# Threshold attention and an ELU layer on one core: 37 score tiles masked on ScalarE, smaller feed-forward pieces, one scheduled block, a new order of the first 45 steps

## The chip, the core and the metric

The kernel runs on one core of one Trainium2 chip. The core has TensorE (PE in the profile; its weight loads are PEld), VectorE (DVE), ScalarE (ACT), GpSimd (POOL) and SyncE (SP), whose queue issues nearly all DMAs. The metric is the device time of one execution in microseconds (us); lower is better. Times in a profile are counted from its first instruction.

## The reference

The inputs are `q`, `k`, `v` of shape (8, 8, 576, 64) in float32, a scalar `tau`, and two weight matrices of 512 x 2048 and 2048 x 512, which arrive in float64.

```python
scores = scale * np.matmul(q, k.transpose(0, 1, 3, 2))
thresh = np.max(scores, axis=-1, keepdims=True) - tau
scores = np.where(scores >= thresh, scores, -1000000000.0)
attn = np.exp(scores - np.max(scores, axis=-1, keepdims=True))
attn = attn / (np.sum(attn, axis=-1, keepdims=True) + 1e-09)
x = np.matmul(attn, v)            # to (4608, 512): batch x position, head x dim
h = x @ w_in
g = np.where(h > 0.0, h, np.exp(np.minimum(h, 0.0)) - 1.0)
out = g @ w_out
```

So each row of scores keeps only what lies within `tau` of its maximum, and a feed-forward layer with an ELU follows.

## The kernel before, in words

**Tiles.** The 64 heads are taken in 32 pairs (`pr`), each pair in five steps `i`: four blocks of 128 query rows for two heads, and a tail step (`i == NC`) that holds the last 64 rows of both heads and counts as one head. A score tile is 128 x 576 in PSUM, in two halves of 288.

**Two blocks.** The first 45 steps (pairs 0 to 8, 81 score tiles) are built by `early_tasks` in one block with an order written out by hand (`tc.manual_schedule()`). The other 23 pairs and most of the feed-forward work follow in a second such block, whose order comes from a clock of its own (`on_pe`, `at`). The second block forms its products by a scheme with seven products for eight (L1466 and L1606).

**One step of the first block.** `scores` (L551, PE) fills the PSUM tile. `max_of` (L600, DVE) takes the negated row maximum. `bound_of` (L604, POOL) makes the threshold. `exp_of` (L614, ACT) writes exp(score - max) to SBUF. `mask_of` (L623, DVE) compares the PSUM tile with the threshold, multiplies by the exponential, writes the weights `w` and adds up their row sum. `total_of` (L631, DVE; L590, ACT, for the steps in `SU_ACT`) and `reciprocal_of` (L637, DVE) give 1/sum, and the weights are scaled on POOL (`normalize`, L596) or, for the heads in `ACT_NORM`, on ACT (L584). The PSUM tile is free after the mask; from step 10 on (`LATE`) there are two tiles, so that each score waits for the masks of the step before.

**Turning.** The weights must be transposed for the product with `v`. Either PE does it in nine 128 x 128 blocks (L640; six in a tail step) with copies on ACT (L656), or, for the steps in `SQUARES`, DVE transposes 32 x 32 squares (L716) and a trip through DRAM (`there`, then `wTa`/`wTb`, issued by SP) does the rest. `values` (L777 and L782) forms attention times `v`; `values_out` (L899) copies it to `xt`. PE also makes transposes of an identity as padding (28 at the start, 16 after the first scores, then 6 to 11 beside the blocks of steps 0, 1, 3, 5 and 7).

**Weights.** 32 pieces of float64 weights are converted: `load_w` (L408, SP), `convert_rest` (L415 on ACT, L432 on POOL for `REST_POOL`), `convert_shift` (L421, DVE), `convert_add` (L427, POOL), `convert_abs` (L437, ACT), `convert_end` (L445, DVE). Sums of `w_in` blocks for the second block are made on DVE or POOL (`make_in`, L1066; POOL for `IN_POOL`).

**Feed-forward work of the first block.** 32 units for the first 512 rows of output: `ffn1` (L940: two groups of four products, 256 columns each; then exp L947 on ACT, minus one L950 on POOL, ELU L954 on DVE) and `ffn2_plain` (L980: four products of 512 columns). Each unit is given out in two halves by `half()`.

**What sets the order.** Each job is a task with a time: a formula of its step plus two entries of the table `MOVED`, one for the kind of job and one for that single job. The jobs are carried out in the order of these times, each after the jobs that it needs (`do`), so that a job with a late time moves forward to the first job that needs it. Every engine then runs its own instructions in that order.

```python
def task(x, t, key, f, *needed):
    each = "_".join(map(str, x)) if isinstance(x, tuple) else x
    made[x] = [t + (MOVED.get(key, 0.0) if key else 0.0) + MOVED.get(each, 0.0), len(made), f, needed, False]
```

Of the kernel before, what the change touches and what calls it, by code (L numbers as in the profile page):

```python
# [18 lines left out]
ACT_NORM = {(0, 1), (10, 0), (10, 1), (11, 1), (13, 0), (15, 1), (16, 0), (17, 0), (17, 1), (18, 1), (22, 0), (24, 0), (25, 0),  # L19
 (26, 1), (28, 0), (30, 1), (31, 0), (32, 0), (33, 0), (35, 0), (36, 0), (36, 1), (37, 0), (40, 1), (44, 0), (44, 1)}  # L20
IN_POOL = {(6, 2), (1, 2), (7, 1), (0, 0), (3, 1), (6, 1), (0, 2), (5, 0), (7, 2), (2, 2), (1, 0), (4, 1), (5, 2)}
SU_ACT = {33, 41, 13, 16, 24, 30}
REST_POOL = {9, 27}

MOVED = {
# [289 lines left out]
def kernel(  # L315
# [642 lines left out]
    def hidden(c, u, n):  # L958
        half, u = divmod(u, NU // 2)
        return gs[c][half][:, u : u + n]  # L960
# [917 lines left out]
```

## Time and profile before

| what | value |
|---|---|
| median of 3 runs | 1300.2 us (1298.6 to 1300.24) |
| profiled execution: span from first to last instruction | 1298.8 us |
| mean granted TensorE clock | 0.997 |
| median of the runs less the span | 1.4 us |
| first product of the second block (L1466) | 282.14 us |
| DMA | 256.01 MB, mean 197 GB/s |

The profiled execution has no time of its own beside its span; the runs' median stands for it, 1.4 us above.

The page gives the busy time of each engine over the span, then rows of 40 slices in which a digit is the busy share in tenths. A group line names the source line, the engine, the operation, out<-in with shape and count, then the busy time, the mean time of one in ns, and the idle time of the engine just before with what ended it. A line of the timeline begins with start and length in us; in square brackets is the wait before it. The share of an engine is an average over stages, so tables of stretches are read beside it: the first block lies in 0 to 282 us.

| 0 to 282 us | PE | DVE | ACT | POOL |
|---|---|---|---|---|
| busy, us | 268.5 | 222.0 | 168.4 | 179.7 |

### The profile page before, as it was taken

Reading aid. Unit: us, or ns where it says so; the run is one execution under the profiler, and the core shown is the slowest. Engines: PE = TensorE matmul, PEld = TensorE weight load, DVE = VectorE, ACT = ScalarE, POOL = GpSimd, SP = SyncE. Lnnn points to the kernel's source line nnn. Section 1 sums busy time; section 2 is a strip of 40 time slices with the busy share of each in tenths; the row PEclk is TensorE's granted clock in tenths of the full one; section 3 lists DMA queues with packets and bytes.
Section 4 is the critical chain, followed back from the end, with each engine's and each line's share of the span. In section 5 each row is a group of like instructions: output and inputs, shape, how many; then the busy total and the mean of one; then the engine's idle time right before and its main releaser. Section 6 shows DMA issues by size and latency. Waiting matters only on the chain.

```text
span 1298.8 us, 21747 instructions
## 1 busy us (share of the span) xinstructions
PE 1277.1 (98%) x6822; PEld 993.8 (77%) x6822; DVE 1011.8 (78%) x2199; ACT 567.9 (44%) x1224; POOL 790.9 (61%) x1181
## 2 busy tenths in 40 slices
PE   9999999899999999999999999999999999999998
PEld 7676576446878888878878787878787888888887
DVE  6787887788888988898889889897989882545534
ACT  5888644335262525353444444353525261421320
POOL 4686645767476756766576757574867473524533
PEclk9999999899999999999999999999999999999999
DMA  7546377879898988899889888899899875222211
GB/s 149 129 146 191 97 192 207 250 203 267 210 255 223 269 226 242 236 269 225 237 214 250 240 235 223 254 245 240 227 255 256 229 214 169 89 73 63 92 61 33
DMA packets 327827, 256.01 MB, mean 197 GB/s; under 512 B 209312, under 2 KB 288672, under 8 KB 327712
## 3 DMA queue, kind: packets, MB, share of 16 engines
q1 hardware_dynamic: 325776, 254.14, 72.1%
q8 instruction: 54, 0.88, 0.3%
q10 hardware_dynamic: 1936, 0.48, 0.2%
q14 instruction: 61, 0.50, 0.1%
HBM read 165.94 MB, written 88.60 MB: 196 GB/s over the span
## 4 chain that ended last, share of the span: by engine, by line
PE 82%; DVE 4%; DMA 2%; issue 1%; POOL 1%; ACT 1%; SPq 0%; DVEq 0%; ACTq 0%; POOLq 0%
PE f L1606 30%; PE f L1466 28%; PE sc L829 7%; PE sc L889 7%; PE f L980 3%; PE sc L551 2%; PE f L940 1%; PE sc L881 1%; DMA there<-x 1%; PE pv L782 1%; PE sc L876 1%; DVE x L716 1%; PE rt L640 1%; DVE w L623 1%; DMA sw<-win_sums 1%
## 5 line engine op out<-in xcount | busy, mean ns | idle before, releaser
L596 POOL TENSOR_SCALAR w<-w,rs 128x576 f32<-128x576 f32 x172 | 141.4, 830 | 78.0 <-DVE rs L637 73.3
L836 DVE TENSOR_REDUCE mx<-sc 128x1 f32<-128x576 f32 x207 | 148.2, 749 | 29.6 <-PE sc L829 25.8
L846 ACT ACTIVATE w<-sc,mx 128x576 f32<-128x576 f32 x115 | 82.9, 740 | 117.9 <-DVE mx L836 99.9
L1466 PE MATMUL f<-xt,sw 128*128 128x256 f32 x512 | 123.9, 384 | 1.4 <-ACT xt L899 0.8
L1466 PE MATMUL f<-xt,w_in_sb 128*128 128x256 f32 x512 | 122.3, 381 | 0.1
L842 POOL TENSOR_SCALAR th<-mx,ntau 128x2 f32<-128x2 f32 (+1 forms) x115 | 34.3, 298 | 136.6 <-DVE mx L836 136.6
L716 DVE STREAM_TRANSPOSE x<-w 128x512 f32<-128x512 f32 (+2 forms) x163 | 106.9, 690 | 11.8 <-POOL w L596 10.6
L1466 PEld LDWEIGHTS f<-xt,sw 128*128 128x128 f32 x512 | 93.6, 190 | 21.6 <-issue 4.9
L1466 PEld LDWEIGHTS f<-xt,w_in_sb 128*128 128x128 f32 x512 | 96.2, 190 | 15.9 <-ACT w L1480 2.8
L1466 PE MATMUL f<-x,w_in_sb 128*128 128x256 f32 x448 | 106.1, 379 | 1.3 <-ACT g L1527 1.3
L1606 PE MATMUL f<-w_out_sb,g 128*128 128x256 f32 x448 | 107.1, 382 | 0.0
L1606 PE MATMUL f<-w_out_sb,s 128*128 128x256 f32 x448 | 107.0, 382 | 0.0
L1606 PE MATMUL f<-t,s 128*128 128x256 f32 x448 | 105.8, 379 | 0.0
L829 PE MATMUL sc<-kT,qT 64*128 64x448 f32 (+4 forms) x736 | 103.2, 416 | 0.5 <-DVE w L850 0.5
L829 PEld LDWEIGHTS sc<-kT,qT 64*128 64x128 f32 x736 | 80.6, 186 | 25.5 <-issue 16.8
L1553 POOL TENSOR_TENSOR s<-g 128x256 f32<-128x256 f32 x104 | 80.4, 778 | 29.3 <-PE f L1606 20.0
L850 DVE SCALAR_TENSOR_TENSOR w<-sc,th,w 128x576 f32<-128x576 f32 x115 | 89.7, 810 | 10.2 <-ACT w L846 10.1
L1466 PEld LDWEIGHTS f<-x,w_in_sb 128*128 128x128 f32 x448 | 85.0, 190 | 13.3 <-ACT g L1527 1.7
L1606 PEld LDWEIGHTS f<-w_out_sb,g 128*128 128x128 f32 x448 | 84.1, 190 | 14.2 <-issue 3.2
L1606 PEld LDWEIGHTS f<-w_out_sb,s 128*128 128x128 f32 x448 | 84.2, 190 | 13.5 <-issue 2.5
L1606 PEld LDWEIGHTS f<-t,s 128*128 128x128 f32 x448 | 85.1, 190 | 11.6
L596 POOL TENSOR_SCALAR e<-e,rs 128x576 f32<-128x576 f32 x92 | 68.5, 748 | 35.5 <-DVE rs L637 33.4
(209 smaller groups left out, 2831.5 us busy)
## 6 DMA issues: line engine op xcount, KB each, us to landing
there<-x SPq DMA_DIRECT2D x436, 144.0 KB, 3.6
wTb<-there SPq DMA_DIRECT2D x56, 576.0 KB, 6.5
wTa<-there SPq DMA_DIRECT2D x53, 576.0 KB, 4.9
sw<-win_sums SPq DMA_DIRECT2D x62, 384.0 KB, 4.3
t<-wout_sums SPq DMA_DIRECT2D x45, 512.0 KB, 5.8
qm<-in_q_dram SPq DMA_DIRECT2D x124, 72.0 KB, 4.8
vm<-in_v_dram SPq DMA_DIRECT2D x64, 128.0 KB, 3.7
wst<-in_moe_w_in_dram SPq DMA_DIRECT2D x16, 512.0 KB, 4.4
```

The lines of the kernel that those rows point to most:

```text
L596: nc.gpsimd.tensor_scalar(wv, wv, st["rs"][:, h : h + 1], 1.0, ALU.mult, ALU.mult)
L716: nc.vector.transpose(x[:, :, c0 : c0 + nc_], src.rearrange("p (c g n) -> p g c n", c=nc_, n=T))
L829: on_banks(nc.tensor.matmul(o, qT[r, i * P : (i + 1) * P], kT[r, k0 : k0 + n], start=True, stop=True, skip_group_check=True), o)
L836: on_banks(nc.vector.tensor_reduce(st["mx"][:, h : h + 1], st["sc", h], axis=AX.XY if i == NC else AX.X, op=ALU.max, negate=True), st["sc" ...
L842: nc.gpsimd.tensor_scalar(st["th"][:, cs], st["mx"][:, cs], -1.0, ntau, ALU.mult, ALU.add)
L846: on_banks(nc.scalar.activation(st["e", h], st["sc", h], AF.Exp, bias=st["mx"][:, h : h + 1]), st["sc", h])
L850: on_banks(nc.vector.scalar_tensor_tensor(st["e", h], st["sc", h], st["th"][:, h : h + 1], st["e", h], ALU.is_ge, ALU.mult, accum_out=st[" ...
L889: on_banks(nc.tensor.matmul(o, vm[:, h, c], parts[part][:, g0:g1, h * (NC + 1) + c], start=False, stop=(c == NC - 1), skip_group_check=Tru ...
L980: nc.tensor.matmul(cur[c, i][:, :DM], hidden(c, ft % NU, 1)[:, 0, ft // NU, i], w_out_sb[:, ft], start=(ft == 0), stop=(ft == NFT - 1))
L1466: nc.tensor.matmul(loc["banks"][place], left[:, j], right[:, j], start=(begins and j == 0), stop=(j == 1), skip_group_check=True)
L1553: engine.tensor_tensor(o, x, y, op)
L1606: nc.tensor.matmul(place(m), lhs, rhs, start=(begins and v == 0), stop=(v == RU - 1), skip_group_check=True)
```

## The change

Sizes of the sets, counted over heads or pieces that exist:

| set | before | after |
|---|---|---|
| `MASK_ACT`: heads masked on ACT | none | 37 of 81 |
| `ACT_NORM`: heads scaled on ACT | 24 | 38 |
| `SU_ACT`: steps summed on ACT | 6 | 12 |
| `REST_POOL`: low words on POOL | 2 | 17 of 32 |
| `SHIFT_POOL`: shifts on POOL | none | 7 of 32 |
| `IN_POOL`: weight sums on POOL | 13 | 14 |
| `SQUARES`: steps turned through DRAM | 17 | 18 (step 22 is new) |

- A head in `MASK_ACT` has no exponential, bound and mask of the old kind. `pivot_of` (DVE) writes th = -max + tau, limited to 104, for each row. `sink_of` (ACT) writes a parametric relu of score + th to SBUF: what is below zero is multiplied by 2^126. `raise_of` (ACT) takes exp(that - tau) in place and adds up the row sum, so that the sunk elements become zero. The next user of the PSUM tile waits for `sink_of`, not for the mask.
- `ffn1` and `ffn2_plain` hand out four parts instead of two; each old place for a half now holds two jobs, `half` and `rest_half`, which move separately.
- The two-head steps turned through DRAM use two DVE transposes (five and four blocks) instead of three.
- The loads of pair 1 leave the start job and become jobs of their own.
- The second block's code moves into the first `manual_schedule` block.
- `MOVED` is new for the jobs of the first block; its entries for the second block are equal in both kernels.
- Code for turning q and k on PE (`QK_PE`) is added, with an empty set: it does nothing.

```diff
+SHIFT_POOL = {0, 2, 3, 4, 13, 24, 29}
+QK_PE = set()
+    DEEP = 104.0
+    STEEP = 2.0**126
...
-        nc.vector.tensor_scalar(ntau, ntau, -1.0, None, ALU.mult)
-        nc.vector.tensor_scalar(ntau0, ntau, 1.0 / SCALE, None, ALU.mult)
+        nc.vector.tensor_scalar(ntau0, ntau, -1.0 / SCALE, None, ALU.mult)
+        nc.vector.tensor_scalar(ntau, ntau, DEEP, -1.0, ALU.min, ALU.mult)
...
-            nc.vector.tensor_scalar(top, hi, 3, None, ALU.logical_shift_left)
+            if i in SHIFT_POOL:
+                nc.gpsimd.tensor_tensor(top.bitcast(I32), hi.bitcast(I32), eight.broadcast_to([P, WN]), ALU.mult)
+            else:
+                nc.vector.tensor_scalar(top, hi, 3, None, ALU.logical_shift_left)
...
+    def pivot_of(pr, i, h):
+        st = open_steps[pr, i]
+        mx, th = st["mx"][:, h : h + 1], st["th"][:, h : h + 1]
+        if pr:
+            nc.vector.tensor_scalar(th, mx, ntau, None, ALU.subtract)
+        else:
+            nc.vector.tensor_scalar(th, mx, keep, ntau, ALU.mult, ALU.subtract)
+
+    def sink_of(pr, i, h):
+        st = open_steps[pr, i]
+        wv = weights_of(st)[:, h * S : (h + 1) * S]
+        nc.scalar.activation(wv.rearrange("p (a n) -> p a n", a=2), st.pop(h)[:, :, :HALF], AF.Prelu,
+                             bias=st["th"][:, h : h + 1], scale=1.0 if pr else keep, alpha=STEEP)
+
+    def raise_of(pr, i, h):
+        st = open_steps[pr, i]
+        wv = st["w"][:, h * S : (h + 1) * S]
+        nc.scalar.activation(wv, wv, AF.Exp, bias=ntau, accum_out=st["sm"][:, h, :1])
...
-        if i < NC and pr >= JOINED:
+        if i < NC:
             turn_part(0, w[:, : (NC + 1) * P], NC + 1)
             turn_part(NC + 1, w[:, (NC + 1) * P :], NC)
-        elif i < NC:
-            turn_part(0, w[:, :MAIN], NC)
-            turn_part(NC, w[:, MAIN : MAIN + P], 1)
-            turn_part(NC + 1, w[:, MAIN + P :], NC)
...
-        def part(k):
+        def part(x):
+            k, j0 = x // 2, x % 2 * 2
             ft = 2 * u + k
-            if k == 0:
+            if x == 0:
                 loc["ph"] = bank()[:, : 2 * CT].rearrange("p (k t) -> p k t", k=2)
-            for j in range(KJ):
+            for j in range(j0, j0 + 2):
...
-        return [lambda: run(0), lambda: run(1)], (done, no, no) if 4 * part + 4 == NFT else (no, no, no)
+        return [lambda k=k: run(k) for k in range(4)], (done, no, no) if 4 * part + 4 == NFT else (no, no, no)
...
             load(0, ("v",))
-            load(1)
             idle(28)
...
-            rooms += [("mask", n, h) for h in hs]
+            rooms += [("exp" if (n, h) in MASK_ACT else "mask", n, h) for h in hs]
...
                         task(("half", n, x, y), t + u, f"half{x}{k}", half)
+                        task(("rest_half", n, x, y), made["half", n, x, y][0] + 0.001, None, half, ("half", n, x, y))
...
     with tc.manual_schedule():
         early_tasks()
-    assert progress[0] == len(pieces) and not units and not pending
-    with tc.manual_schedule():
+        assert progress[0] == len(pieces) and not units and not pending
         need_extra("in")
```

More of the change, by code (lines that the diff above doesn't have):

```diff
@@ L398 @@
     staged, tops = {}, {}
+    eight = const.tile([P, 1], I32, name="eight")
+    nc.gpsimd.memset(eight, 8)
     progress = [0]
@@ L460, in load @@
             m = tiles[name]
+            if pr in QK_PE:
+                if "ends" not in tiles:
+                    tiles["ends"] = wstage.tile([TAIL, 2, 2, D], FP32, name="ends", bufs=1)
+                both, blocks = src[b, 2 * j : 2 * j + 2], blocks_of(pr, name[0])
+                for i in range(2):
+                    queue.dma_start(blocks[:, :, i], both[i, :MAIN].rearrange("(c p) d -> p c d", p=P))
+                queue.dma_start(tiles["ends"][:, int(name == "km")], both[:, MAIN:].rearrange("i p d -> p i d"))
+                continue
             for i, d in pieces:
@@ L479, in load_v, with room_q @@
             nc.sync.dma_start(vd[r, r], vh[MAIN:])
-    def prep_q(pr):
+    def room_q(pr):
         if pr < 2:
@@ L495, in prep_k, with blocks_of, turn_blocks, turn_last @@
     def prep_k(pr):
-        kT = pairs[pr][1] = firsts[pr] if pr < 2 else qkp.tile([P, TAIL + S], FP32, name="kT")
+        kT = room_k(pr)
         nc.vector.transpose(kT[:, TAIL:], raws[pr]["km"].rearrange("p j d -> p (j d)"))
+    def blocks_of(pr, name):
+        return raws[pr][name + "m"].rearrange("p j d -> p (j d)")[:, :MAIN].rearrange("p (c i d) -> p c i d", i=2, c=NC)
+    def turn_blocks(pr, name):
+        rt, src = psum["t"].tile([P, NC, P], FP32, name="rt", tag="rt"), blocks_of(pr, name)
+        for c in range(NC):
+            transpose(rt[:, c], src[:, c].rearrange("p i d -> p (i d)"))
+        return rt
+    def turn_last(pr):
+        rt, ends = psum["t"].tile([P, NC, P], FP32, name="rt", tag="rt"), raws[pr]["ends"]
+        for x in range(2):
+            nc.tensor.matmul(rt[:, x, :TAIL], ends[:, x], idents[-1][:TAIL, :TAIL], is_transpose=True, skip_group_check=True)
+        return rt
+    def copy_blocks(pr, name, rt):
+        rt = rt.rearrange("p c n -> p (c n)")
+        if name == "q":
+            nc.scalar.mul(room_q(pr)[:, :MAIN], rt, keep)
+        else:
+            nc.scalar.copy(room_k(pr)[:, TAIL:S], rt)
+    def copy_last(pr, rt):
+        qT, kT, _ = pairs[pr]
+        nc.scalar.mul(qT[:, MAIN:], rt[:, 0, :TAIL], keep)
+        nc.scalar.copy(kT[:, S:], rt[:, 1, :TAIL])
     def copy_q(pr):
@@ L954, in elu @@
             nc.vector.scalar_tensor_tensor(loc["g"], loc["g"], 0.0, loc["ph"], ALU.min, ALU.max)
-        return [lambda: part(0), lambda: part(1)], (exp, minus, elu)
+        return [lambda x=x: part(x) for x in range(4)], (exp, minus, elu)
     def hidden(c, u, n):
@@ L978, in run @@
                 cur[c, i] = bank()
-            for ft in range(4 * part + 2 * k, 4 * part + 2 * k + 2):
-                nc.tensor.matmul(cur[c, i][:, :DM], hidden(c, ft % NU, 1)[:, 0, ft // NU, i], w_out_sb[:, ft],
-                                 start=(ft == 0), stop=(ft == NFT - 1))
+            ft = 4 * part + k
+            nc.tensor.matmul(cur[c, i][:, :DM], hidden(c, ft % NU, 1)[:, 0, ft // NU, i], w_out_sb[:, ft],
+                             start=(ft == 0), stop=(ft == NFT - 1))
         def done():
@@ L1184, in early_tasks @@
             made["prep", x, 0] = made["copy", x, 0] = made["start"]
-            made["load", x, 1] = made["start"]
-        made["v", 0] = made["v", 1] = made["start"]
+            task(("load", x, 1), -99.0, None, lambda x=x: load(1, (x + "m",)), "start")
+        made["v", 0] = made["start"]
+        task(("v", 1), -98.0, None, lambda: load(1, ("v",)), "start")
         task("rest", begin[0] + 0.5, "restq", rest_of_q, "start")
@@ L1190, in early_tasks @@
         made["v", 2] = made["v", 3] = None
+        turned = {}
         for pr in range(1, NPAIR + 6):
@@ L1290, in early_tasks @@
-                exps.append(("exp", n, h))
                 back = ("turned", n - (2 if last_ else WBUFS)) if n >= WBUFS else None
-                task(("mask", n, h), at_(2.0 + 1.6 * h, 5.6 + 0.1 * h, 4.0 + 0.1 * h), f"mask{h}{k}", lambda pr=pr, i=i, h=h: mask_of(pr, i, h),
-                     ("exp", n, h), ("th", n, h), ("mask", n, 0) if h else back, "late" if last_ else None)
+                t_exp, t_th, t_mask = (at_(0.3 + 0.7 * h, 2.0 + 0.6 * h, 1.0 + 0.5 * h), at_(0.4 + 0.7 * h, 2.2 + 0.6 * h, 1.1 + 0.5 * h),
+                                       at_(2.0 + 1.6 * h, 5.6 + 0.1 * h, 4.0 + 0.1 * h))
@@ new lines, in early_tasks @@
+                if (n, h) in MASK_ACT:
+                    task(("exp", n, h), t_exp, f"exp{h}{k}", lambda pr=pr, i=i, h=h: sink_of(pr, i, h), ("th", n, h), back, "late" if last_ else None)
+                    task(("th", n, h), t_th, f"th{h}{k}", lambda pr=pr, i=i, h=h: pivot_of(pr, i, h), ("max", n, h))
+                    task(("mask", n, h), t_mask, f"mask{h}{k}", lambda pr=pr, i=i, h=h: raise_of(pr, i, h), ("exp", n, h))
+                else:
+                    task(("exp", n, h), t_exp, f"exp{h}{k}", lambda pr=pr, i=i, h=h: exp_of(pr, i, h),
+                         ("max", n, h), exps[-1] if exps else None, ("mask", *exps[-2][1:]) if len(exps) > 1 else None)
+                    task(("th", n, h), t_th, f"th{h}{k}", lambda pr=pr, i=i, h=h: bound_of(pr, i, h), ("max", n, h))
+                    exps.append(("exp", n, h))
+                    task(("mask", n, h), t_mask, f"mask{h}{k}", lambda pr=pr, i=i, h=h: mask_of(pr, i, h), ("exp", n, h), ("th", n, h),
+                         ("mask", n, 0) if h and (n, 0) not in MASK_ACT else back, "late" if last_ else None)
```

65 lines of the change are left out of this document (46 added, 19 removed), and 581 rows, old and new, of the table MOVED.

## The prediction

> **What bounds the kernel now.** I read the head of the page first, then the table of stretches, then the timeline where a stretch was not full.
>
> ```profile
> span 1298.8 us, 21747 instructions
> PE 1277.1 (98%) x6822; PEld 993.8 (77%) x6822; DVE 1011.8 (78%) x2199; ACT 567.9 (44%) x1224; POOL 790.9 (61%) x1181
> ...
> PE   9999999899999999999999999999999999999998
> ...
> PEclk9999999899999999999999999999999999999999
> ```
>
> TensorE (PE) is busy 98% of the span, and the two slices below 9 are the eighth (its clock dips there too) and the last. So a gain must come from TensorE time that is idle, slow or filled with padding. The stretches (columns: span; busy time of PE, PEld, DVE, ACT, POOL; clock; DMA share; GB/s) say where that is:
>
> ```profile
> 0.00:60.00 60.00, 56.16 (x388) 42.43 (x389) 45.19 (x106) 39.23 (x75) 33.46 (x68) 1.00 0.67 140
> 60.00:220.00 160.00, 157.24 (x800) 103.69 (x799) 128.66 (x283) 108.80 (x223) 99.13 (x147) 1.00 0.59 167
> 220.00:282.00 62.00, 55.05 (x204) 25.31 (x202) 48.19 (x111) 20.41 (x35) 47.06 (x71) 0.94 0.82 222
> 282.00:320.00 38.00, 35.49 (x172) 26.01 (x172) 33.58 (x73) 20.82 (x48) 28.50 (x43) 1.00 0.89 243
> 320.00:1298.80 978.80, 973.10 (x5263) 796.41 (x5262) 756.16 (x1629) 378.68 (x846) 582.79 (x856) 1.00 0.74 202
> ```
>
> The changed job list runs from 0 to 282 us, where the first L1466 product starts. By busy time TensorE is idle there only 3.8 + 2.8 + 7.0 = 13.6 us. But matmul records overlap: in an unbroken run of the timeline 56 products of 256 columns take 12.29 us, 0.219 each, while one record lasts 0.38. So I counted work by the pace from start to start: L980 128 x 0.43 = 55.0; L940 256 x 0.216 = 55.3; scores 36 x 1.17 + 9 tail steps x 0.97 = 50.8; values 44.4 (9 x 1.88 and 8 x 2.30 for L782, 9.2 for L777); turned blocks 234 x 0.109 = 25.5; first L876 1.2. That is 232.2 us of work in 282.1: **49.9 us are not work**. Of these 14.4 are the 132 padding transposes at 0.109 (28 of them before any score), some 3 the half clock at 242.6 to 249.4, and about 32 gaps: some 9 in 0 to 60 (4 of them the start), 10 in 60 to 220, 13 in 220 to 282. No other engine is full: over 0 to 282 DVE is busy 222, ACT 168, POOL 180.
>
> The largest gap:
>
> ```profile
> 238.07 1.24 PE L551 MATMUL sc<-kT,qT 64*128 64x288 f32 x8
> ...
> 243.31 2.26 PE L551 MATMUL sc<-kT,qd 128*128 128x288 f32 x4 [4.00 <-DVE w L623]
> ```
> ```profile
> 239.00:243.30 4.30, 0.31 (x4) 0.02 (x1) 3.79 (x8) 2.05 (x3) 2.90 (x6) 0.92 0.99 333
> 243.30:249.00 5.70, 5.69 (x9) 3.06 (x10) 4.12 (x12) 0.74 (x1) 5.25 (x6) 0.50 0.89 198
> ```
>
> Scores of step 38 are followed at once by those of step 39, whose PSUM tile is freed by the mask (L623) of step 38, 5.0 us after its scores began. TensorE waits 4.0 us, and then its granted clock is 0.50 for the next 5.7 us. The price of this one place is 4.0 + some 3 = **7 us**.
>
> **The change, part by part.** Durations:
>
> ```profile
> L623 DVE SCALAR_TENSOR_TENSOR w<-sc,th,e 128x576 f32<-128x576 f32 x81 | 63.7, 812 | 18.2 <-ACT e L614 9.6 <-POOL th L604 6.8 <-POOL qd L504 0.6
> L614 ACT ACTIVATE e<-sc,mx 128x576 f32<-128x576 f32 x72 | 51.2, 742 | 37.7 <-DVE mx L600 37.6
> L427 POOL TENSOR_TENSOR wtop<-wtop,wst 128x512 int32<-128x512 int32 x32 | 42.8, 1338 | 11.0 <-DVE wtop L421 5.7 <-ACT wTb L656 1.9 <-ACT wst L415 1.2
> L604 POOL TENSOR_SCALAR th<-mx,ntau 128x1 f32<-128x1 f32 x81 | 24.2, 303 | 30.7 <-DVE mx L600 30.2
> L421 DVE TENSOR_SCALAR wtop<-wst 128x512 uint32<-128x512 uint32 x32 | 16.9, 538 | 0.1
> L584 ACT ACTIVATE w<-w,rs 128x576 f32<-128x576 f32 x24 | 18.5, 774 | 17.5 <-DVE rs L637 15.2 <-DMA km<-in_k_dram 2.3
> ```
>
> *37 masks on ScalarE.* Each drops a DVE mask (0.812 and its accumulator read 0.083) and a POOL bound (0.303); it adds a DVE pivot (128x1, as L379: 0.155) and a second ACT pass. No row shows Prelu; I take L614's 0.742 for it, the same shape from PSUM; ends are 0.59 (L947, 128x512) and 0.83 (L614 of the first pair, with a scale from memory). The Exp in SBUF I take as L584's 0.774, up to 1.06 if a read of the accumulator as long as L590's 0.29 comes with it. DVE: 37 x (0.155 - 0.895) = -27.4. POOL: -11.2. ACT: 37 x 0.774 = +28.6 (ends +23 and +43).
> *Shifted between engines.* ACT_NORM grows from 24 real heads to 38: ACT +14 x 0.774 = +10.8, POOL -14 x 0.843 = -11.8. Fifteen more low words on POOL: ACT -15 x 0.687 = -10.3, POOL +15 x 0.673 = +10.1. Seven shifts: DVE -3.8, POOL +9.4 (as L427; 0.7 to 1.5 each as ends). Six more sums on ACT, one more weight sum on POOL: DVE -1.4, ACT +1.8, POOL +0.8.
> *Squares.* One more step (22) is turned through DRAM: TensorE -9 x 0.109 = -1.0, ACT -1.4, DVE +1.5, four more stores and one fetch while the DMA share is 0.6. Two transposes for three in the 14 two-head steps: DVE 14 x (0.838 + 0.682 - 1.635) = -1.6.
> Sums over 0 to 282: DVE 222 to 189, ACT 168 to 198 (192 to 212), POOL 180 to 177. This work lies beside TensorE, so none of it counts by itself. Cover: TensorE's 232 us; without it, ACT's 198 would be the longest. What counts is when PSUM and turned weights come free.
>
> *When PSUM comes free.* A score tile is now held through max, exp and mask; for the 37 heads only through max, pivot and Prelu. That is one pass of 0.8 us less, and no wait for the POOL bound (L623 waits 6.8 us for it in all). Queued behind a late Prelu on ACT are norms, PSUM copies (L656) and the ELU's exp; behind a late pivot, the next maxima.
>
> *Order and quarter units.* The matmuls are the same; a unit's piece is 0.86 us instead of 1.72. I sorted the jobs by the formulas and offsets of both tables. Before, no feed-forward piece stands between scores 38 and 39; after, four do (3.4 us). That leaves 0.6 of the 4.0 us and keeps the clock. After also puts two to nine pieces around nearly every score from step 10 on. Bare spots stay: only values (2.5 to 2.9 us with their first product) stand between scores 29 and 30, 34 and 35, 39 and 40, 43 and 44, and between 7 and 8.
>
> *Loads of pair 1* leave the start job; they are on SP's queue still, behind those of pair 0, and scores of step 2 start at 16.2 us: nothing (ends -1 to +1). *Single block:* the first wide score at 280.63 waited for a mask, no engine drains there: nothing (ends -2 to +2). The second block's 171 offsets are equal in both tables, so the 978.8 us from 320 on stay.
>
> **Sum.** (a) The place at 239: 7 us at most; its four pieces leave other places, so at least the clock's 3: I take 6. (b) Other gaps of 220 to 282, 5 to 6 us, every step there waiting for its predecessor's mask; 7 of the heads of steps 37 to 44 change: 1.5 (0 to 5). (c) 60 to 220, 10 us in gaps of 0.2 to 0.7: finer pieces, fewer waits for masks: 3 (0 to 8). (d) 0 to 60, 5 us and 11 of padding behind the first scores: 1.5 (0 to 8). (e) Transposes 1. Together 13, bounds 4 to 29. From the profiled span 1298.8 that gives 1285.8. The runs' median, 1300.2, lies 1.4 above the span: **1287 us**. About 0.2% (2.6 us) is what a measurement of this kernel tells from no change.
>
> **Rivals.**
> 1. *ACT takes DVE's place (17%).* In 40 to 140 ACT is busy 84 of 100 us. In steps 7 to 23 it gains 11 masks (+9.4) and 7 norms (+5.4) and loses 13 low words (-8.9): 90 of 100. As its queue is in order, PSUM copies would then come late and (b), (c), (d) vanish, 6 us: 1293. Against it: in that stretch ACT still has 10 us.
> 2. *A new bare spot (slower, 13%).* The values that alone cover scores 29-30, 34-35, 39-40, 43-44 need a fetch of 3.9 to 5.4 us to have landed; where one is late by 1 us or more, the 3.8 us from a score's end to the next free tile stay open, the clock halves, and the place costs 7 us. One or two are paid by the 13; from the third the kernel is slower; with three or four it stands at 1300.2 - 13 + 21 to 28 = 1308 to 1315. The limit of the clock lies between 1.5 us (the wait before 307.08 left it at 1.00) and 4.0. For it: exactly this happened at 239. Against it: the wait for a fetch is 0.3 us at most now. The Trainium skill, TensorE: Matmul & The Clock Gate, section Part 1, puts the limit at an idle window of about 3.4 us; by that, waits of 3.8 us would halve the clock as assumed here, while by the upper row, 4.0, such a place would cost 3.8 us alone and four would be needed.
> 3. *Prelu and Exp need different tables (slower, 3%).* The trace has one table load, 1.283 us, for Exp, Tanh and copies together. Two loads for each of 37 heads are 95 us on ACT, 200 + 95 = 295 in a stretch of 282, at a busy share of 0.9 some 328: 46 more and no gain, 1346. The Trainium skill, ScalarE: Activation LUTs, section Table sets, says that cheap functions such as relu are in every set, and that each switch costs about 2.7 us with its drain (estimate from that page: 200 us on ACT); no run here shows Prelu yet.
> 4. *More than I take (15%).* DVE's 33 us and the earlier tiles close most gaps: -20 to -25, 1275 to 1280.
> 5. *Moved, not closed (7%).* Gaps of equal size elsewhere: 1298 to 1303. That the masks do not move is excluded by the sets in the diff.
> Forecast itself: 45% (1281 to 1292, its own range). Faster by over 0.2%: 45 + 15 + 17 = 77%; within 7%; slower 16%. The range 1275 to 1308 takes in rivals 1, 4 and 5 and the near end of 2; it leaves out the rest of 2, rival 3 and gains over 25 us, some 15%.
>
> **What would show it.** The first L1466 product at about 269 us instead of 282; no stretch of half clock after the start; L623 44 times instead of 81; DVE near 189 us of that stage and ACT near 200; one table load. Wrong: a wait of TensorE over 3 us, a PE row below 9 between slices 3 and 9, or ACT over 90% where score tiles are late.

## The result and the profile after

The changed kernel takes 1289.3 us (median of 4 runs, 1288.85 to 1290.47) against 1300.1 (median of 4, 1298.6 to 1300.24): a ratio of 0.9921 with a 95% interval of 0.9907 to 0.9935, faster by 10.8 us. The forecast was 1287.0, in a range of 1275 to 1308. The profiled execution of the new kernel took 1289.09 us with a span of 1287.3; in what follows times inside a span come from such profiled executions, and ratios from the runs.

The head of the page of the new kernel, the same lines as those shown of the old one:

```profile
span 1287.3 us, 21652 instructions
...
PE   8999999989999999999999999999999999999998
...
PEclk9999999999999999999999999999999999999999
```

The clock row has no dip left, and the eighth slice is a 9; the first and the ninth are an 8 now. The stretches with the same columns as before (span; busy PE, PEld, DVE, ACT, POOL; clock; DMA share; GB/s), cut at the first product of the second block again, which is L1580 here:

```profile
0.00:60.00 60.00, 55.29 (x380) 42.12 (x381) 41.87 (x99) 41.18 (x79) 36.27 (x68) 1.00 0.60 130
60.00:220.00 160.00, 159.54 (x811) 105.40 (x810) 117.92 (x255) 128.64 (x271) 102.90 (x139) 1.00 0.67 184
220.00:271.00 51.00, 48.09 (x195) 23.00 (x194) 41.33 (x86) 29.21 (x55) 35.92 (x50) 1.00 0.86 256
...
309.00:1287.30 978.30, 972.36 (x5262) 796.09 (x5260) 755.33 (x1627) 378.76 (x845) 582.10 (x855) 1.00 0.74 202
```

The first L1580 product starts at 270.18 instead of 282.14, and from it to the end it takes 1017.1 us against 1016.7 before: everything that was gained lies ahead of it. In the first row TensorE is busy less than before (55.29 against 56.16): the start did not gain. The gap at 239 us is closed by four quarter pieces, and the step behind it follows without a wait:

```profile
232.32 1.24 PE L617 MATMUL sc<-kT,qT 64*128 64x288 f32 x8
233.49 3.70 PE L1065 MATMUL f<-w_out_sb,g 128*128 128x512 f32 x8
237.03 1.13 PE L617 MATMUL sc<-kT,qd 128*128 128x288 f32 x4
```

The groups of the mask (busy us in all, mean ns of one, then idle time before and its releasers):

```profile
L711 DVE SCALAR_TENSOR_TENSOR w<-sc,th,e 128x576 f32<-128x576 f32 x44 | 34.9, 813 | 14.2 <-ACT e L704 10.6 <-POOL th L670 2.5 <-POOL g L1035 0.3
L695 ACT ACTIVATE w<-w,ntau 128x576 f32<-128x576 f32 x37 | 28.7, 776 | 0.9
L689 ACT ACTIVATE w<-sc,th 128x576 f32<-128x576 f32 x33 | 24.3, 738 | 18.1 <-DVE th L682 11.5 <-POOL t L1178 2.9 <-DVE x L804 2.2
L682 DVE TENSOR_SCALAR th<-mx,ntau 128x1 f32<-128x1 f32 x33 | 7.0, 213 | 1.1
L695 ACT ACTIVATION_READ_ACCUMULATOR w<-w,ntau 128x1 f32 x37 | 7.0, 190 | 0.0
```

L689 is the parametric relu: 738 ns, where 742 was taken. The second pass, L695, is 776 ns plus 190 for the read of its accumulator. The pivot, L682, is 213 ns, where 155 was taken.

To see where the 12 us come from, I worked out from the traces how much TensorE time is lost in each stretch of steps: the time from one matmul's start to the next, less the shortest usual time (the tenth percentile in the old and the new kernel) for that pair of shapes. The half clock counts as lost, too. Two executions of one kernel (new and e11) differ by up to 1.1 us in a column, and another rule for pairs that are rare moves most entries by less than 0.5 us (the last of e9 by 0.9). For old and new and for the experiments below (us; the right column is the start of the first product of the second block):

| kernel | steps 0-9 | 10-22 | 23-34 | 35 to the first product | first product at |
|---|---|---|---|---|---|
| old | 12.2 | 8.8 | 6.6 | 17.9 | 282.1 |
| new | 13.0 | 5.2 | 5.6 | 9.5 | 270.2 |
| e1 code only | 11.8 | 8.8 | 6.6 | 16.4 | 281.1 |
| e2 masks alone | 21.8 | 12.1 | 19.1 | 22.9 | 312.7 |
| e3 order alone | 22.1 | 13.3 | 25.1 | 22.2 | 320.2 |
| e4 old engine split | 22.0 | 29.6 | 17.2 | 22.6 | 328.6 |
| e5 old, half moved | 12.3 | 8.5 | 6.5 | 15.1 | 279.2 |
| e6 new, bare spot | 12.3 | 5.4 | 5.4 | 14.7 | 273.8 |
| e7 whole halves | 13.9 | 12.3 | 11.2 | 11.9 | 285.7 |
| e8 early table load | 11.9 | 5.6 | 5.4 | 14.3 | 273.1 |
| e9 old, wait filled | 11.9 | 8.6 | 6.2 | 12.3 | 279.8 |
| e10 e8, end filled | 12.6 | 5.5 | 5.4 | 8.7 | 269.3 |
| e11 new again | 12.6 | 5.6 | 5.4 | 10.6 | 270.1 |
| e12 ten masks back | 21.6 | 10.2 | 5.4 | 10.7 | 283.6 |

In e9 and e10 unread transposes fill 3.5 and 1.5 us of wait; this table does not count them as lost.

### The profile page after: what moved, and what is told of

Its sections match the earlier page's. It is cut to its first block, busy times and chain, and to the rows that moved or that the text cites. A ratio compares the mean times of both kernels' runs of the same rounds, so it can differ in the third digit from the quotient of the medians.

```text
span 1287.3 us, 21652 instructions
## 1 busy us (share of the span) xinstructions
PE 1270.5 (99%) x6813; PEld 992.2 (77%) x6813; DVE 989.9 (77%) x2136; ACT 598.5 (46%) x1296; POOL 788.5 (61%) x1154
## 4 chain that ended last, share of the span: by engine, by line
PE 87%; DVE 5%; ACT 2%; DMA 2%; POOL 2%; issue 1%; SPq 1%; DVEq 0%; ACTq 0%; POOLq 0%
PE f L1720 30%; PE f L1580 28%; PE sc L913 7%; PE sc L973 7%; PE f L1025 4%; PE sc L617 3%; PE rt L728 2%; PE pv L866 2%; PE sc L965 1%; DVE x L804 1%; PE sc L960 1%; PE f L1065 1%; DMA wst<-in_moe_w_out_dram 1%; DVE mx L666 1%; DMA sw<-win_sums 1%
## 5 line engine op out<-in xcount | busy, mean ns | idle before, releaser
L662 POOL TENSOR_SCALAR w<-w,rs 128x576 f32<-128x576 f32 x158 | 127.7, 817 | 80.4 <-DVE rs L725 77.1
L1580 PE MATMUL f<-xt,sw 128*128 128x256 f32 x512 | 123.9, 384 | 1.2 <-ACT xt L983 0.5
L1580 PE MATMUL f<-xt,w_in_sb 128*128 128x256 f32 x512 | 122.3, 381 | 0.1
L804 DVE STREAM_TRANSPOSE x<-w 128x512 f32<-128x512 f32 (+1 forms) x151 | 107.6, 744 | 17.3 <-POOL w L662 16.2
L1580 PEld LDWEIGHTS f<-xt,sw 128*128 128x128 f32 x512 | 93.7, 190 | 21.3 <-issue 5.5
L1580 PEld LDWEIGHTS f<-xt,w_in_sb 128*128 128x128 f32 x512 | 96.2, 190 | 15.9 <-ACT w L1594 2.8
L1580 PE MATMUL f<-x,w_in_sb 128*128 128x256 f32 x448 | 106.1, 379 | 1.6 <-ACT g L1641 1.6
L1667 POOL TENSOR_TENSOR s<-g 128x256 f32<-128x256 f32 x104 | 80.3, 778 | 29.6 <-PE f L1720 20.1
L934 DVE SCALAR_TENSOR_TENSOR w<-sc,th,w 128x576 f32<-128x576 f32 x115 | 89.8, 811 | 10.3 <-ACT w L930 10.2
L1580 PEld LDWEIGHTS f<-x,w_in_sb 128*128 128x128 f32 x448 | 85.0, 190 | 13.5 <-ACT g L1641 2.0
L1720 PEld LDWEIGHTS f<-w_out_sb,s 128*128 128x128 f32 x448 | 84.2, 190 | 13.5 <-issue 2.5
```

The source lines that it names most:

```text
L662: nc.gpsimd.tensor_scalar(wv, wv, st["rs"][:, h : h + 1], 1.0, ALU.mult, ALU.mult)
L804: nc.vector.transpose(x[:, :, c0 : c0 + nc_], src.rearrange("p (c g n) -> p g c n", c=nc_, n=T))
L934: on_banks(nc.vector.scalar_tensor_tensor(st["e", h], st["sc", h], st["th"][:, h : h + 1], st["e", h], ALU.is_ge, ALU.mult, accum_out=st[" ...
L1580: nc.tensor.matmul(loc["banks"][place], left[:, j], right[:, j], start=(begins and j == 0), stop=(j == 1), skip_group_check=True)
L1667: engine.tensor_tensor(o, x, y, op)
L1720: nc.tensor.matmul(place(m), lhs, rhs, start=(begins and v == 0), stop=(v == RU - 1), skip_group_check=True)
```

## The experiments

### Each part by itself

**e1_code_only.** The new code with the old tables; ACT_NORM, IN_POOL, SU_ACT, REST_POOL and the order, MOVED, are those of the old kernel, too:

```diff
-MASK_ACT = {(0, 0), (0, 1), (5, 1), (7, 1), (8, 0), (9, 1), (13, 0), (15, 0), (15, 1), (16, 0), (20, 0), (20, 1), (23, 0),
...
+MASK_ACT = set()
-SHIFT_POOL = {0, 2, 3, 4, 13, 24, 29}
+SHIFT_POOL = set()
```

> The new code with the old tables: no mask on ScalarE, the old sets of engines, every second half right behind its first half, the old order of jobs, and pieces 1 and 2 of nine value groups transposed in one issue of two parts. My theory, in which the gain comes from the new order and the new split of the engines together: only the transposes are left, which I priced at 1.0 us; the time lies between the old 1300.1 and 1298.5, the wait of 4 us and the half clock at 239 us stay. Rival, that code outside the tables carries much of the gain: 1296 or less.

Measured: 1302.83 us, ratio to the old kernel 1.0014 (1.0005 to 1.0022), slower than either expectation. VectorE's two transposes for three bring nothing: from step 2 to step 39 no step starts more than 0.2 us from its old place, and scores 39 start at 243.3 us as in the old kernel. The 1.0 us that the expectation speaks of is not tried here: the prediction put it on the nine blocks of step 22 that TensorE no longer turns, and with the old tables e1 turns step 22 on TensorE as before (1388 matmuls ahead of the second block, as in the old kernel; the new one has 1379). What the profile shows ahead of the second block (1.1 us) comes behind step 39, where the half clock lasted 3.41 us instead of 6.83; and the second block takes 1.8 us longer than in the old kernel, half of it in its first 300 products. So the code outside the tables carries none of the gain.

**e2_masks_alone, e3_order_alone, e4_old_engine_split.** Three ways to take the change apart. e2 is e1 with the new set of 37 masks left in. e3 is the new kernel with this edit:

```diff
-MASK_ACT = {(0, 0), (0, 1), (5, 1), (7, 1), (8, 0), (9, 1), (13, 0), (15, 0), (15, 1), (16, 0), (20, 0), (20, 1), (23, 0),
...
+MASK_ACT = set()
```

e4 is the new kernel with ACT_NORM, IN_POOL, SU_ACT and REST_POOL of the old one and

```diff
-SHIFT_POOL = {0, 2, 3, 4, 13, 24, 29}
+SHIFT_POOL = set()
```

> The same old tables and old order, with the 37 masks on ScalarE alone. VectorE gets about 28 us of work less in 45 steps (813 ns each) and 37 pivots more (213 to 273 ns), ScalarE 36 us more (738 to 776 ns and a 190 ns read each). If VectorE's place in the queue was what the old order suffered from, the time falls by 2 to 6 us (1294 to 1298) with the order as it was. If the order is what counts, and the masks only move the load, the old order, made for masks on VectorE, now waits for ScalarE at places where its Exp and copies stand ahead: 1300 to 1308.

> The new order, the new sets and the quarter units, but all 90 masks on VectorE again. VectorE's load up to the first product of the second block goes from 201 to about 222 us of 270, ScalarE's from 199 to about 163. Theory that masks on ScalarE are what makes the new order possible: products wait for masks again, 1295 to 1305. Rival, that the order of TensorE's pieces alone closes the gaps and VectorE keeps up: within 1.5 us of 1289.3.

> The new kernel with the old choice of engines for normalisations, additions, sums, copies and shifts (seven shifts, fifteen of the seventeen rests back on VectorE or ScalarE); masks and order of TensorE's pieces as in the new one. Theory that the 37 masks and the order carry it: 1289 to 1293. Rival, that the freed time of VectorE is needed twice (moves to GpSimd included): more than 1294, with waits for VectorE between 150 and 270 us.

Measured: 1330.16 us, ratio 1.0221 (1.0205 to 1.0236); 1338.78, 1.0291 (1.0272 to 1.0309); 1353.66, 1.0398 (1.0383 to 1.0413). e2 and e3 end far above what was expected (1308 and 1305 at most; the expectation of e3 speaks of 90 masks, but there are 81). For e4 the rival came, more than 1294, but TensorE waited for GpSimd most of all, and not for VectorE. Against the old kernel each part without the others costs 29 to 53 us, some three to five times what all of them together gain. What TensorE waited for in the first 290 us, with the sum, the number of waits and the longest; masks alone first:

```profile
PE rt L716 <- POOL w L650: 10.1, 11, 2.9
PE sc L605 <- ACT w L677: 6.8, 4, 4.0
PE rt L716 <- ACT wTb L732: 3.8, 2, 2.0
```

the new order without the masks on ScalarE:

```profile
PE rt L726 <- POOL w L660: 14.3, 6, 6.3
PE sc L615 <- DVE w L709: 9.4, 8, 2.7
PE sc L615 <- POOL qT L530: 3.1, 1, 3.1
```

the old split of the engines:

```profile
PE rt L727 <- POOL w L661: 17.4, 12, 5.0
PE rt L727 <- ACT w L649: 4.6, 3, 2.1
```

and the new kernel itself, in its 270 us:

```profile
PE rt L728 <- POOL w L662: 1.5, 2, 1.3
PE rt L728 <- POOL ident masks.py:199: 1.5, 1, 1.5
PE sc L617 <- DVE w L711: 1.4, 2, 1.3
```

No engine is full in any of them (with the masks alone, ScalarE is busy 197 us of the 313 ahead of the second block, VectorE 200, GpSimd 167). As I read these rows, what is long is the chain from a mask to the scaled weights that the transposes (`rt`) read: mask, sum, reciprocal, scaling on GpSimd. In each variant one link of it comes at another time than the order of the queues allows for. The order was not fitted anew to any of the three, so they show what a part costs in an order made for another split, and not what it could gain in an order of its own.

**e12_ten_masks_back** shows such a place by itself, and whether the loss is made good later.

```diff
-MASK_ACT = {(0, 0), (0, 1), (5, 1), (7, 1), (8, 0), (9, 1), (13, 0), (15, 0), (15, 1), (16, 0), (20, 0), (20, 1), (23, 0),
+MASK_ACT = {x for x in {(0, 0), (0, 1), (5, 1), (7, 1), (8, 0), (9, 1), (13, 0), (15, 0), (15, 1), (16, 0), (20, 0), (20, 1), (23, 0),
...
-  0), (34, 0), (35, 1), (36, 1), (37, 0), (37, 1), (38, 1), (40, 0), (41, 0), (42, 0), (44, 0)}
+  0), (34, 0), (35, 1), (36, 1), (37, 0), (37, 1), (38, 1), (40, 0), (41, 0), (42, 0), (44, 0)} if x[0] >= 20}
```

> The new kernel with the ten masks of steps 0 to 16 back on VectorE, the other 27 on ScalarE. With all 37 back the kernel was 49 us slower, 1.3 us for each, while VectorE got only 21 us of work. Theory that a loss is local and is kept (TensorE has no slack later): some 13 us are lost by step 17, as in that run, and stay: 1300 to 1304. Rival, that the later steps catch up because their order had room: 1291 to 1296.

Measured: 1304.14 us against 1290.12 of the unchanged kernel on the same chip (ratios to the old kernel 1.0041, 1.0029 to 1.0054, and 0.9927): 14 us for ten masks, whose passes on VectorE are some 8 us. It is lost where the masks are, 2.3 us by step 8, 7.9 by step 9 and 12.6 by step 17, and it is still 13.5 at the first product of the second block: nothing is made good. GpSimd's timeline of this run, between the scores of steps 8 and 9:

```profile
47.83 0.74 POOL L662 TENSOR_SCALAR w<-w,rs 128x576 f32<-128x576 f32 x1
49.65 0.63 POOL L670 TENSOR_SCALAR th<-mx,ntau 128x1 f32<-128x1 f32 x1 [1.07 <-DVE mx L666]
50.24 0.64 POOL L456 TENSOR_SCALAR wst<-wst 128x512 f32<-128x512 uint32 x1
50.97 1.27 POOL L451 TENSOR_TENSOR wtop<-wtop,wst 128x512 int32<-128x512 int32 x1
52.23 2.71 POOL L662 TENSOR_SCALAR w<-w,rs 128x576 f32<-128x576 f32 x3
```

The same queue in the unchanged kernel (e11):

```profile
42.80 0.74 POOL L662 TENSOR_SCALAR w<-w,rs 128x576 f32<-128x576 f32 x1 [0.93 <-PE sc L617]
43.51 0.27 POOL L670 TENSOR_SCALAR th<-mx,ntau 128x1 f32<-128x1 f32 x1
43.74 0.67 POOL L456 TENSOR_SCALAR wst<-wst 128x512 f32<-128x512 uint32 x1
44.49 1.29 POOL L451 TENSOR_TENSOR wtop<-wtop,wst 128x512 int32<-128x512 int32 x1
45.77 2.20 POOL L662 TENSOR_SCALAR w<-w,rs 128x576 f32<-128x576 f32 x3
```

The jobs look alike, but the bound (L670) is another one. In the unchanged kernel it is that of step 7, whose maximum is there already. With (8, 0) masked on VectorE again, the first head of step 8 has a bound, too, and that is the one that stands ahead of the two conversions and the scalings of step 7: it waits for the maximum of step 8, which needs the scores of step 8 (47.52 us). So the scalings of step 7, whose reciprocals are there at 48.84, start at 52.23, and TensorE's timeline shows what follows:

```profile
53.55 1.31 PE L728 MATMUL rt<-ident,w 128*128 128x128 f32 x5 [3.91 <-POOL w L662]
55.32 1.54 PE L728 MATMUL rt<-ident 128*128 128x128 f32 x6 [0.46 <-ACT wTb L744]
```

From scores 8 to scores 9 it takes 11.2 us instead of 5.5, the half clock for 3.41 us behind the wait among it. By this reading one tiny instruction (0.27 us in the unchanged kernel) in the wrong place of one queue costs 5.7 us; no run moves it alone.

**e7_whole_halves.** The quarters out of the order:

```diff
-    91.1, "rest_9": 97.1, "rest_half_10_1_0": -81, "rest_half_10_2_0": -4, "rest_half_11_1_0": -1, "rest_half_11_2_0":
...
+    91.1, "rest_9": 97.1, "s13.0": -0.93,
```

All 68 entries of that kind are out, so that a half's second part follows its first.

> The new kernel with the second part of each feed-forward half right behind its first part (68 entries of the order taken out), so that the units are halves again. Theory, in which the quarter unit is a finer filling: some waits grow by up to half a piece each, 1290 to 1294. Rival, that the quarters are what closes the place at 239 us and the period of 5.1 us at scores 40 to 43: 1295 or more, with a wait of over 2 us there. Third, that they are idle detail: within 0.7 us of 1289.3.

Measured: 1302.46 us, ratio 1.0019 (1.0008 to 1.0029). The whole gain is gone. This is the second rival in size, but not by its place: the lost time of steps 35 to the first product rises by 2.4 us, and that of steps 10 to 34 from 10.8 to 23.5, where the old kernel loses 15.4. So in this order the gain of the middle steps cannot do without the quarter unit. An order made anew for whole halves was not tried.

### The place at 239 us and the clock

**e5_before_half_moved.** In the old kernel:

```diff
-    "half_38_0_0": -3.1,
+    "half_38_0_0": 1.90,
```

> The old kernel with one feed-forward half (1.72 us of products) moved from ahead of scores 38 to between scores 38 and 39, where TensorE waited 4.0 us. My theory: the wait falls to about 2.3 us, the clock record of 0.5 (6.8 us) at 242.6 us is gone, and the time falls by the 1.7 us of cover and the 3.4 us that half the clock cost, less what the earlier scores 38 lose: 1295 to 1297. Rival, that the half clock has another cause than the bare wait: the record stays and the time falls by 1.7 us at most, 1298.4 or more.

Measured: 1298.69 us against 1300.04, ratio 0.9989 (0.9979 to 1.0). In the profiled execution the wait is 2.09 us, no record of half clock follows and the first product comes 3.0 us earlier; the runs give only 1.4 us. Five of the eleven executions took 1297.07 to 1297.40 us, the profiled one among them, and six 1298.69 to 1300.9, so the 3.0 us are not what each of them gains. The mechanism of the theory is there, and its size is nearer to the rival's.

**e6_after_bare_spot.** The converse in the new kernel:

```diff
-    "post_35_1_0_1": 854.29,
+    "post_35_1_0_1": 871.79,
...
-    "post_36_1_0_2": 851.8,
+    "post_36_1_0_2": 863.40,
```

> The new kernel with the four quarter pieces (3.70 us) that stand between scores 38 and 39 moved behind scores 39, nothing else. The spot is bare again: scores 39 wait for the mask of scores 38, by its end in the new profile some 3.2 us. Theory (a bare wait of some 3 to 4 us brings half the clock for 6.8 us): a wait of 2.5 to 3.5 us, the clock record of 0.5 behind it, 1292 to 1295. Rival, that the pieces moved behind the scores fill the later gaps and the clock holds: 1289 to 1292, no record under 1.0.

Measured: 1293.12 us, ratio 0.9940 (0.9927 to 0.9952), against 0.9921 and 0.9927 (each plus or minus 0.0013) of the new kernel: some 2 us. The bare spot is back, with ScalarE's mask as its end now:

```profile
231.15 1.24 PE L617 MATMUL sc<-kT,qT 64*128 64x288 f32 x8
235.56 2.29 PE L617 MATMUL sc<-kT,qd 128*128 128x288 f32 x4 [3.18 <-ACT w L689]
237.65 5.35 PE L1065 MATMUL f<-w_out_sb,g 128*128 128x512 f32 x8
```

The wait is 3.18 us, half clock follows for 6.83 us (eight products take 5.35 us instead of 3.70), and the first product comes 3.6 us later. The moved pieces stand behind scores 39 and shorten later gaps, so 3.2 + 3.4 us did not all add up.

**e9_before_filled_wait** parts the wait from the clock. In the old kernel, ahead of scores 39:

```diff
-        return lambda: values_out(pr, part, pv)
...
+        held[:] = [pv]; return lambda: values_out(pr, part, pv)
...
-            task(("sc", n), t + 0.2 if late_ else t - 2.6 if i in (2, NC) else t - 2.0, f"sc{k}", lambda pr=pr, i=i, hs=hs: scores(pr, i, hs), ("prep", "q", pr),
+            task(("sc", n), t + 0.2 if late_ else t - 2.6 if i in (2, NC) else t - 2.0, f"sc{k}", lambda n=n, pr=pr, i=i, hs=hs: ([transpose(held[0][:, :P], idents[-1]) for _ in range(30 * (n == 39))], scores(pr, i, hs)), ("prep", "q", pr),
```

(`held` keeps the tile of the value products that was copied last; the transposes go there.)

> The old kernel with 30 transposes that nobody reads put ahead of scores 39, where TensorE waited 4.0 us bare (one takes some 0.12 us, so 3.7 us); nothing else is moved. This parts the wait from the half clock. Theory: scores 39 start at 243.3 us as before, since the mask ends when it did, but no clock record of 0.5 follows, and scores 40 start some 3.4 us earlier, at 248.1; in all 1296.5 to 1297.5. Rival, that the clock is not tied to the bare wait, or that transposes do not hold it: record and time as before, 1299.5 to 1301.

Measured: 1299.14 us against 1299.59, ratio 0.9998 (0.9989 to 1.0007): no change that the runs can tell, though the interval leaves room for a gain of 1.4 us. The wait at 239 us and what follows, in stretches of 3.41 us, with the columns of the stretches above, in the old kernel:

```profile
239.16:242.57 3.41, 0.15 (x2) 0.00 (x0) 3.06 (x6) 1.89 (x3) 2.19 (x6) 1.00 1.01 328
242.57:245.99 3.42, 2.68 (x5) 1.85 (x6) 2.04 (x7) 0.00 (x0) 3.34 (x4) 0.50 0.88 284
```

and in this run:

```profile
238.57:241.98 3.41, 3.35 (x30) 3.11 (x29) 3.28 (x6) 1.66 (x3) 2.42 (x6) 1.00 1.00 332
241.98:245.40 3.42, 2.90 (x9) 1.67 (x10) 2.29 (x8) 0.74 (x1) 3.34 (x5) 1.00 0.89 259
```

The transposes hold the clock at 1.00, as the theory has it. But what TensorE does faster runs into the next wait, as its timeline in this run shows:

```profile
242.50 1.21 PE L551 MATMUL sc<-kT,qd 128*128 128x288 f32 x4 [0.58 <-DVE w L623]
...
249.02 1.79 PE L551 MATMUL sc<-kT,qT 64*128 64x288 f32 x8 [1.27 <-DVE kT L497]
```

Scores 40 wait 1.27 us for VectorE's transposed keys. From scores 39 to scores 40 it takes 6.5 us instead of 8.2, so 1.7 of the 3.4 us that half the clock cost TensorE are left. In this execution, the shortest of the eleven, the first product of the second block comes 2.4 us earlier, 0.8 of them gained ahead of scores 39. What the runs of the old kernel show beside it agrees in size: of its 53 executions on the three chips of these experiments, the 26 with a mean granted clock of 0.997 or less took on the average 1.6 us longer than the 27 with more, each counted from the median of its chip; where the clock was halved in them is not on record. So I estimate that the half clock costs the kernel 1 to 2 us at most, and not 3.4.

### The start and the end of the stage

**e8_early_table_load.** In the start job, behind the loads:

```diff
             load(0, ("v",))
+            nc.scalar.activation(seen, ident[:, :1], AF.Exp)
             idle(28)
```

> The new kernel with one Exp of 128 by 1 elements added on ScalarE right after the loads at the start, whose output nothing uses. Theory: the load of the activation table (1283 ns), which now stands at 9.72 us behind the wait of the first parametric relu, runs during the loads of the start, the first mask ends 1.3 us earlier, and the start to scores 2 gains 0.5 to 1.3 us of which some is eaten later: 1288.0 to 1289.0. Rival, that the first steps are held by the loads of pair 1 and not by the first mask: no change, 1289.3 within 0.4.

In the new kernel the load of the activation table stands behind the wait of the first parametric relu. ScalarE's timeline of the new kernel:

```profile
9.72 1.28 ACT L689 ACT_TABLE_LOAD   x1 [9.72 <-DVE th L684]
11.01 1.55 ACT L689 ACTIVATE w<-sc,th,keep 128x576 f32<-128x576 f32 x2
```

and of this run:

```profile
9.39 1.80 ACT L689 ACTIVATE w<-sc,th,keep 128x576 f32<-128x576 f32 x2 [5.60 <-DVE th L684]
```

Measured: 1291.00 us, ratio 0.9928 (0.9916 to 0.9941), the same as without it; both expectations, 1289.7 at most, were missed. The start did gain. In the profiled executions of the new kernel and of e8, e10 and e11 the first scores start anywhere between 6.3 and 7.5 us, with the early load or without it, so I count from them: scores 2 follow after 11.2 us in e8 and e10, after 12.1 in the new kernel and e11, a gain of 0.9 us. Scores 44 still start 1.5 us earlier than in the new kernel and 1.2 earlier than in e11. The end took it back: the value products at 264 us waited 4.1 us for a fetch of turned weights, with half clock behind, where the new kernel waited 1.3.

**e10_early_load_filled_end.** With 12 unread transposes in that wait:

```diff
-                    room_for("t", lambda: do(("out", pr, part)))
+                    room_for("t", lambda: do(("out", pr, part))); [transpose(held[0][:, :P], idents[-1]) for _ in range(12 * ((pr, part) == (8, 0)))]
                     got.append(values(pr, part))
```

> The new kernel with the early Exp, and 12 unread transposes (1.5 us) ahead of the value products that waited for a DMA at 264 us (4.1 us in the run with the early Exp alone, with half clock behind it). The wait itself stays. Theory: the half clock behind that wait is gone, 1.7 us less than in the disturbed executions with the early Exp: 1288.5 to 1290, the spread smaller. Rival: the DMA lands when it lands, and what came earlier by 1.2 us at the start is lost there whatever the clock does: 1290 to 1291.5.

**e11_new_again.**

> The new kernel unchanged, for comparison on the same chip as the two before: 1289.3 within 1 us.

Measured on one chip: 1289.21 us, ratio 0.9924 (0.9912 to 0.9937), and 1290.12, ratio 0.9927 (0.9915 to 0.9940). No half clock in the profile of e10, the first product 0.8 us earlier, and the runs cannot tell the two apart. Where the 0.8 us go is to be seen on VectorE's timeline, here of e10:

```profile
290.80 1.44 DVE L804 STREAM_TRANSPOSE x<-w 128x640 f32<-128x640 f32 x2 [1.51 <-DMA there<-x]
```

and of e11:

```profile
290.71 1.44 DVE L804 STREAM_TRANSPOSE x<-w 128x640 f32<-128x640 f32 x2 [0.80 <-POOL ge L1620]
```

In e10 the tile that this transpose writes is free when a store of the step before has landed, at 290.8 us; in e11 VectorE waits for GpSimd until 290.71. The maxima, the Exp and the copies behind it follow within 0.1 us of each other in both (TensorE goes on at 295.92 and 295.84). So in these two executions what arrives earlier at the second block waits there for a store. No version measured here beats the new kernel by more than the measurement can tell.

## Why the prediction was right, and which of its terms were not

The sign, the place and the sum held; the terms erred in both directions and made each other good, so it is in part luck that the sum came so near. By the table of lost time, of the 12.0 us that the first product moved:

- **(a) The place at 239 us**, taken as 6: 5.2 us of lost time when it is opened again (e6, 14.7 against 9.5; 4.1 against e11's 10.6), but only 3.6 at the first product and some 2 in the runs; and 1.4 (e5) or nothing that the runs can tell (e9) when it is closed by itself in the old kernel. The mechanism was right: where the wait is filled, no half clock follows (e9). The term was mis-sized because the price was added up on TensorE alone: the prediction took something off for the wait, whose pieces come from other places, and nothing off the clock's 3 us, and with the clock held the next thing to be late was VectorE's `kT`, 1.27 us.
- **(b) Other gaps from step 35 on**, taken as 1.5: with e6's 14.7 against the old 17.9, 3.2.
- **(c) Steps 10 to 34**, taken as 3: 15.4 to 10.8, so 4.6 (4.4 with e11's 11.0). Without the quarter units it is gone (23.5, e7).
- **(d) The start**, taken as 1.5: no gain, 0.8 us worse (0.4 in e11's profile and 0.1 in e6's, whose starts are the same). Two things stood there that the prediction had left out or counted as nothing. The table load moved behind the first wait of ScalarE (1.28 us; in e8 scores 2 come 0.9 us sooner after the first scores). And the transposes of pair 1 moved on VectorE behind the masks of step 1: they start at 17.73 us instead of 12.98, and scores 2 follow at 19.4 instead of 16.2. The second was read from the traces and not tried.
- **(e) The nine blocks of step 22**, taken as 1.0: they are gone from the new kernel (1379 matmuls ahead of the second block instead of 1388), but the time that the table does not count as lost is the same in both (282.1 less 45.5 is 236.6, 270.2 less 33.3 is 236.9), so nothing of it shows in the sum. No run tries this term by itself; e1 does not.

By these, -0.8 + 4.6 + 3.2 + 5.2 is 12.2, near the 12.0 of the traces. (b) is read from the table alone: no run opens those gaps by themselves. The work of the engines came out near the forecast for ScalarE (199 us up to 271 us, against 198) and GpSimd (175 against 177), and less well for VectorE (201 against 189), where the 37 pivots alone were 2.4 us dearer than taken.

Of the rivals, the fourth (1275 to 1280) and the fifth (1298 to 1303) are excluded by the time, and the third by the trace: one table load stands in it for Exp, Tanh, copies and the parametric relu together. The Trainium skill, ScalarE: Activation LUTs, section Table sets, says that cheap functions such as relu and copy are in every set. The trace agrees for the copies, and it shows the same of the parametric relu, which that section does not name. The first and the second did not happen in this change, but both are there as soon as a part of it is missing. With the masks alone ScalarE does take VectorE's place (`sc <- ACT w`, 6.8 us in four waits); the prediction priced that at 6 us, and with what follows it was 29. And waits with half clock behind them appear in every one of e2, e3, e4, e6, e7 and e12. What gave the forecast its place was the reading of both tables of the order, job by job, at 239 us, though that place is worth less than half of the gain; it was not the load of the engines, in which nothing is full in e2 and e4 either.

Of the signs that the prediction named, the first product (270.18 us, for about 269), the 44 masks, the clock, ScalarE's load and the one table load came as it said. One of its signs of being wrong came, too: the ninth slice of the PE row is an 8. TensorE is busy 28.9 of the 32.2 us there and waits 1.25, 1.31 and 0.69 us at the end of the first block and the beginning of the second. The kernel was faster all the same, so that sign was too strict.

What stays open: which of the order's shifts between steps 10 and 34 carry the 4.6 us (only the quarter units as a whole were taken out), what (b) and (e) are worth by themselves, and why the transposes of pair 1 had to move.

## What to carry to other kernels

Where every queue is in order and the order is written out by hand, an order and a split of work among engines are fitted to each other: take a part of such a change alone and it can cost several times what the whole gains, with no engine full. So read such a change by the chain from one result to its reader and by what stands ahead in each queue at that time, not by sums of busy time. And price a stall only after asking what the freed engine waits for next: of 7 us on TensorE at one place, some 2 were the kernel's.

## What the runs showed of the hardware beyond that

- **The clock goes by fixed windows.** In all fourteen traces the clock's records begin on a grid of 3.413 us, counted from the first. Sorted by how busy TensorE was in a window at full clock (5238 windows, the end of each span left out), the next window was at half clock in 13 of 13 where the share was under 0.3, in 15 of 22 from 0.3 to 0.5, in 5 of 57 from 0.5 to 0.7, and never in 5146 above. The Trainium skill, TensorE: Matmul & The Clock Gate, section Part 1, tells of a free-running window of 3413 ns and of an idle one before the clock falls; the grid agrees, but the window need not be idle. So the same wait may or may not halve the clock, as it falls into one window or over two: a wait of 4.1 us in e8 stood over two windows (0.46 and 0.34 busy) and only the second was followed by half clock. And a wait of 1.90 us (e4, up to 212.19) was followed by half clock, while one of 2.95 us (e10, up to 295.92) was not. So no single number between 1.5 and 4.0 us, such as the prediction sought, is the limit. (Its lower one, before 307.08, is 1.35 us in the trace.)
- **The accumulator of ScalarE** costs 190 ns per read beside the pass (VectorE's: 82), 7.0 us here.
- **A factor read from memory** makes the parametric relu 828 ns instead of 738, about as much more as with Exp (833 and 740).
- **The table load stands where its instruction waits.** In the old kernel it ran at 2.30 us, hidden by the loads; in the new one it came behind a wait of 9.72 us, and an activation with nothing to wait for brought it forward again (e8).
